# A fused linear-attention and MoE kernel: the last token tile evicted in halves by two engines, and another load time in the planner

## The chip, the cores and the metric

The kernel runs on one core of a Trainium2 chip. The metric is the device time of one execution in microseconds; less is better. The time before is the median of three runs.

## The reference, cut to what matters

```python
def _attn_ref(q, k, v, alpha):                 # each (4, 8, 768, 48): batch, heads, positions, head size
    state = np.zeros((B, H, D, D))
    for t in range(S):
        state = alpha[:, :, t, :, None] * state + np.einsum('bhd,bhe->bhde', k[:, :, t], v[:, :, t])
        y[:, :, t] = np.einsum('bhd,bhde->bhe', q[:, :, t], state)
    return y

x = attn_out.transpose(0, 2, 1, 3).reshape(3072, 384)   # tokens x (heads * head size)
h = np.maximum(x @ w_in, 0.0)                           # w_in: 384 x 2048
out = (h * h) @ w_out                                   # w_out: 2048 x 384, out: 3072 x 384 float32
```

A gated linear recurrence over 768 positions for 4 x 8 heads, and behind it a two-layer network with a squared ReLU over the 3072 tokens.

## The kernel before

**Tiles.** The 3072 tokens are 24 chunks of 128 positions, six per batch (NT = 24, NCH = 6). A chunk goes through the recurrence in closed form: the logarithm of alpha (tile `L_s`), its running sum by a matmul with a triangle of ones, the exponentials `A` and `Ainv` of it, `qA_s` = q * A and `kI_s` = k * Ainv, their transposes `qkT`, the scores `sc` (all pairs of positions), the masked scores `sm`, and the output as scores times `vb` (v in bf16) plus q times the state `sb` carried from the chunk before; `st` is that state in PSUM. The output is cast to `xn`, transposed, and lies as `xT_big` for the network. There, `w_in` matmuls fill a bank, ScalarE makes `r` = max(h, 0), VectorE squares it into `gT`, and 16 `w_out` matmuls in four quarters make one output tile, which is evicted from its bank into `ob` and stored.

The first four chunks are treated as two "super" pairs (`add_super`, u = 0 and 1), which interleave even and odd positions of 256, so that 64 rows of each of two chunks stand in one tile. The rest go through `add_chunk`, `add_scores` and `add_back`. `add_moe1` and `add_moe2` make the network; its groups of chunks have the sizes GN = 4, 1, 1, 2, 2 and so on.

**What sets the order.** Each step is an `Op` with an engine (or a choice of engines), a duration that the author gives it, the steps it depends on, a priority, and the PSUM bank that it takes and the step that gives the bank back. `Plan.run` is a list scheduler: it walks through time with these durations, and each engine takes the ready step that can start first, by priority among equals. The steps are then sorted by planned start and their instructions emitted in that order. Each engine's instruction stream is that order, and on the chip each engine works it off in order, waiting on semaphores where a tile is not ready. So a planned duration never changes how long something takes; it changes what stands ahead of what.

Loads are steps on a queue "DMA" of the plan, which is first in, first out; a load of 128 x 384 float32 takes `LD` there and is ready 2.4 us later. Stores are steps on "OUT". All loads and stores are issued by SyncE, in the one planned order. A store of a whole tile gets `.late = OUT_LATE`, 3.5 us: this is added to its planned start, so that it stands in SyncE's queue behind loads that are planned up to 3.5 us later:

```python
            op.start = t + getattr(op, "late", 0.0)
...
        self.order.sort(key=lambda o: o.start)
```

TensorE gets dummy matmuls on the tile `warm` where the plan leaves it idle near the start; the last of them stand near 22.9 us. The helper lines L251 (`mm`) and L254 (`tr`) record every matmul and transpose, L365 and L367 are ScalarE's and VectorE's branch of the helper `cast`. In `add_super`, `e_p3a` adds q times the state to the output bank `py`, `e_p3b` adds the masked scores times v, and `add_tail` casts and transposes the result.

Of the kernel before, what the change touches and what calls it, by code (L numbers as in the profile page):

```python
# [8 lines left out]
FP32 = mybir.dt.float32  # L9
# [47 lines left out]
def after(op, x=0.0):  # L57
    return (op, x)
# [86 lines left out]
def kernel(  # L145
# [10 lines left out]
    nc = tc.nc  # L156
    B, H, S, D = q.shape
    HD = H * D
    P = 128
    DP = 64  # L160
    NP = H // 2
    NCH = S // P
    d_model, d_ff = moe_w_in.shape
# [3 lines left out]
    NT = n_tok // P  # L167
# [5 lines left out]
    out_r = out.rearrange("(tt p) n -> tt p n", p=P)  # L173
# [11 lines left out]
    opool = ctx.enter_context(tc.tile_pool(name="opool", bufs=6))  # L185
# [8 lines left out]
    HF = P // 2  # L194
# [6 lines left out]
        out=utri_f, in_=ones_f, compare_op=ALU.is_ge, fill=0.0,  # L201
# [4 lines left out]
        out=sutri_f, in_=ones_f, compare_op=ALU.is_ge, fill=0.0,  # L206
# [10 lines left out]
    for src, dst in ((utri_f, half_in), (sutri_f, half_ex)):  # L217
        nc.vector.memset(dst, 0.0)
        for ab in range(2):
            h = slice(ab * HF, ab * HF + HF)  # L220
            nc.vector.tensor_copy(dst[h, h], src[h, h])
    for ab in range(2):
        h = slice(ab * HF, ab * HF + HF)
# [23 lines left out]
    def pin(ins):  # L247
        tc.keep_in_program_order(ins)

    def mm(*a, **kw):  # L250
        pin(nc.tensor.matmul(*a, **kw))  # L251
# [4 lines left out]
    plan = Plan()  # L256
# [5 lines left out]
    SUP_BANKS = sl_bank[0:4]  # L262
# [3 lines left out]
    def psum(op, shape, dt):  # L266
        i = op.slot.bank
        return banks[i].tile(shape, dt, name=f"bank{i}")
    X_SLACK = 0.2
    LD = 1.05  # L270
    LD2 = 1.51
    WLD = 2.05
    SQ_PRIO = 0.0
# [1 line left out]
    def add(eng, dur, emit, *deps, **kw):  # L275
        return plan.add(Op(eng, dur, emit, deps, **kw))
# [50 lines left out]
    LEAD = 3.5  # L327

    NS = 2
    SIDE = 1  # L330
    EITHER, SLOW = {"DVE": 0.47, "POOL": 0.95}, {"POOL": 0.95}
    KI_ON = [[EITHER, EITHER], [EITHER, EITHER]]
    ST_PRIO = -12.0
    SUP = [dict() for _ in range(NS)]

    def add_load(s, nm):
# [9 lines left out]
        prev = C[s - LB]["use_" + nm] if s - LB >= 2 * NS else None  # L346
        if 2 * NS <= s < 2 * NS + LB and (k - LB // 2) < NS:
            prev = SUP[k - LB // 2]["use_" + nm]
        d["ld_" + nm] = add("DMA", LD, ld, prev, lat=2.4)

# [12 lines left out]
    def cast(op, out_t, in_t):  # L363
        if op.eng == "ACT":
            pin(nc.scalar.copy(out_t, in_t))  # L365
        elif op.eng == "DVE":
            pin(nc.vector.tensor_copy(out_t, in_t))  # L367
        else:
            pin(nc.gpsimd.tensor_copy(out_t, in_t))

    def add_tail(s, done, first, g):
        d = C[s]

        def e_xn():
            d["xn"] = work.tile([P, HD], BF16, name="xn")
            cast(xn, d["xn"], d["py"][:, 0:HD])
        xn = add("ACT", 0.36, e_xn, done, **g)
        first.gives = xn

        def e_p4():  # L380
            d["px"] = psum(p4, [P, KT, P], BF16)
            for j in range(KT):
                tr(d["px"][:, j, :], d["xn"][:, j * P:(j + 1) * P], ident_bf)
        p4 = plan.add(Op("PE", 0.165, e_p4, [xn], takes=GLA_BANKS, lat=0.14, **g))

        def e_xT():
            cast(xT, xT_big[:, :, s * P:(s + 1) * P], d["px"])
        xT = add({"ACT": 0.36, "DVE": 0.27} if s < EARLY else "DVE", 0.27, e_xT, p4, prio=-9.0)
        d["x"] = d["end"] = xT
        p4.gives = xT  # L390
# [176 lines left out]
    def add_super(u):  # L567

        d = SUP[u]
        i = 2 * u % NBUF  # L570
        pair = (C[2 * u], C[2 * u + 1])
        L, qA, kI, ae = L_s[:, i:i + 2], qA_s[:, i:i + 2], kI_s[:, i:i + 2], ae_s[:, i:i + 2]
        old = [C[2 * u - NBUF + ab].get("end") for ab in range(2)] if u >= 2 else []
        g = dict(prio=-10.0 + u * 0.02)
        any_ = (0, 1)
# [11 lines left out]
        vb = [add("POOL", 0.55, lambda t=t: e_vb(t), d["ld_vt"], *old, prio=-5.0) for t in any_]  # L587
# [57 lines left out]
        cq = add({"DVE": 0.61, "ACT": 0.92}, 0, lambda: e_cp(cq, "qT", "pq"), p1q, **g)  # L645
# [33 lines left out]
        sm = []  # L679
# [4 lines left out]
        before = p2  # L684
# [18 lines left out]
        for ab in any_:  # L703
            s = 2 * u + ab
            c = pair[ab]
            r = slice(HF * ab, HF * ab + HF)
            before = C[s - 1].get("sb") if s else None
            if s < NCH - 1:
                def e_ps(c=c, r=r, s=s):
                    if s == 0:  # L710
                        state["ps"] = ps_st.tile([P, NP, 2 * D], FP32, name="st")
                    st = c["st"] = state["ps"]
                    for t in any_:
                        for p in range(NP):
                            mm(st[:, p, :], lhsT=kI[r, t, 2 * p:2 * p + 2, :], rhs=d["vb"][t][r, 2 * p:2 * p + 2, :],
                               start=(s == 0 and t == 0 and p == 0), stop=True, skip_group_check=True)
                ps = plan.add(Op("PE", 0.35, e_ps, [*mk, *vb, ae1, before], lat=0.16, **g))

                def e_stm(c=c, ab=ab):
                    st4 = c["st"].rearrange("p n (j e) -> p n j e", j=2)  # L720
                    pin(nc.vector.tensor_mul(st4, st4, bcast(ae[:, ab], D)))  # L721
                stm = add("DVE", 0.47, e_stm, ps, ae1, prio=ST_PRIO)

                def e_sb(c=c):
                    c["sbt"] = work.tile([P, NP, 2 * D], BF16, name="sb")
                    pin(nc.scalar.copy(c["sbt"], c["st"]))
                c["sb"] = add("ACT", 0.37, e_sb, stm, prio=-12.0)

            def e_p3a(c=c, r=r, s=s, ab=ab):
                c["py"] = psum(c["p3a"], [P, 512], FP32)  # L730
                for p in range(NP):
                    mm(c["py"][:, 2 * p * D:2 * (p + 1) * D], lhsT=d["qT"][:, p, ab].rearrange("k t c -> k (t c)"), rhs=C[s - 1]["sbt"][:, p, :],
                       start=(p == 0), stop=False, skip_group_check=True)

            def e_p3b(c=c, r=r, s=s):
                if s == 0:
                    c["py"] = psum(c["p3b"], [P, 512], FP32)
                for x in any_:
                    for hh in range(2):
                        for p in range(NP):  # L740
                            h = 2 * p + hh
                            mm(c["py"][:, h * D:(h + 1) * D], lhsT=d["sm"][x][r, hh, p, :], rhs=d["vb"][x][r, h, :],
                               start=(s == 0 and x == 0 and hh == 0 and p == 0), stop=(x == 1), skip_group_check=True)
            p3a = None
            if s:
                p3a = c["p3a"] = plan.add(Op("PE", 0.2, e_p3a, [cq, before], takes=SUP_BANKS, **g))
            p3b = c["p3b"] = plan.add(Op("PE", 0.5, e_p3b, [*sm, *vb, after(p3a)], takes=None if s else SUP_BANKS,
                                         lat=0.15, **g))
            add_tail(s, p3b, p3a or p3b, g)

    GN = [4, 1, 1, 2, 2, 2, 2, 2, 2, 2, 2, 2]
    assert sum(GN) == NT
    GT = [sum(GN[:i]) for i in range(len(GN))]
# [51 lines left out]
    def add_moe2(g, tt, before, box, quarters, pools):  # L805

        for qd in quarters:
            def e_mm(qd=qd):
                if qd == 0:
                    box["po"] = psum(box["first"], [P, 512], FP32)[:, 0:d_model]  # L810
                for kf in range(qd * FT // NQ, (qd + 1) * FT // NQ):
                    mm(box["po"], lhsT=gT[g][:, kf, tt * P:(tt + 1) * P], rhs=w_out_b[:, kf, :],
                       start=(kf == 0), stop=(kf == FT - 1))
            fs = range(qd * FT // NQ, (qd + 1) * FT // NQ) if g == 0 else range(FT)
            deps = [o for f in fs for o in sq[(g, f)]] + [w_dep("o", fs[-1] if g == 0 else FT - 1)] + ([after(before)] if before else [])
            op = plan.add(Op("PE", 0.65, e_mm, deps, takes=pools if qd == 0 else None, prio=0.1))
            op.moe = (2, 2.56 / NQ)
            if qd == 0:
                box["first"] = op
            op.lat = 0.05  # L820
            before = op
        if quarters[-1] < NQ - 1:
            return op

        def e_ev():
            box["ob"] = opool.tile([P, d_model], FP32, name="ob")
            if ev.eng == "DVE":
                pin(nc.vector.tensor_copy(box["ob"], box["po"]))
            else:
                pin(nc.scalar.copy(box["ob"], box["po"]))  # L830
        ev = add({"DVE": 0.47, "ACT": 0.38}, 0, e_ev, op, prio=-15.0)
        box["first"].gives = ev

        def e_out():
            s = GT[g] + tt
            if s >= 2 * NS:
                pin(nc.sync.dma_start(out=out_r[s], in_=box["ob"]))
            else:
                for t in range(2):
                    pin(nc.sync.dma_start(out=out2_r[s, t], in_=box["ob"][HF * t:HF * t + HF]))  # L840
        add("OUT", 0.55, e_out, ev, at=0.0).late = OUT_LATE
        return op
# [96 lines left out]
```

## Time and profile before

| | |
|---|---|
| runs shown | 189.12, 188.58, 189.08 us; median 189.08 |
| profiled execution | 187.66 us, of which the span of the core is 185.9 us |
| granted TensorE clock | 0.999 |
| TensorE matmul / weight load | 178.4 / 134.1 us busy |
| VectorE / ScalarE / GpSimd | 133.8 / 122.6 / 29.6 us busy |
| loads of 192 KB | 80, each 3.7 to 4.0 us from issue to landing (median) |
| stores of 192 KB | 20, 2.3 us; in the last 16 us 1.9 us |
| HBM | 25.17 MB read, 4.72 MB written |

The profiled execution is one run of the program under the hardware profiler; its times are counted from the start of the span. A busy time is the sum of an engine's instructions; the end of a matmul is modelled, so TensorE's holes of less than about 0.15 us do not show in it. A line "A <- B: 1.4, 2, 1.0" in the waits says that A waited for B 1.4 us in total, in 2 places, 1.0 at most. A line of the timeline is the start, the length, the engine and line, the output and inputs, and how many instructions of the kind stand together; in brackets is the idle time before it and who ended it. In a line of the groups the numbers behind the bar are the busy time in us, the mean of one in ns, and the idle time before.

### The profile page before, as it was taken

To read this page: it belongs to the slowest core of one execution; us is meant where nothing else is said; L and a number is where in the kernel's file an instruction comes from. 1 tells how busy PE (TensorE), PEld (TensorE's weight loads), DVE (VectorE), ACT (ScalarE), POOL (GpSimd) and SP (SyncE) were. 2 spreads that over 40 slices of the span, in tenths; PEclk is the share of its full clock that TensorE was granted. 3 is DMA by queue.
4 is the path that set the end of the run, shared out by engine and by line. 5 is a ranking of instruction groups with operands and counts; after the bars stand their busy time and mean duration, and the time that the engine had idled before them with its cause. 6 is when DMAs were issued, how large, how long until landed. Compare 5 with 4: busy or idle time off the path is not lost.

```text
span 185.9 us, 5105 instructions
## 1 busy us (share of the span) xinstructions
PE 178.4 (96%) x2037; PEld 134.1 (72%) x2037; DVE 133.8 (72%) x280; ACT 122.6 (66%) x282; POOL 29.6 (16%) x47
## 2 busy tenths in 40 slices
PE   6889899999999999999999999999999999999992
PEld 2666684667887878878878878777868778767761
DVE  7688679875999986876976966866987976842400
ACT  3577779455896896776676776667778668434621
POOL 5044777411012111111020020020020000000000
PEclk9999999999999999999999999999999999999999
DMA  5999999899899999999997984691011011011112
GB/s 146 261 280 339 385 370 331 175 223 205 161 206 209 236 199 231 184 231 201 189 222 162 216 166 101 157 212 61 0 42 46 2 48 42 4 42 42 46 43 84
DMA packets 99176, 30.22 MB, mean 163 GB/s; under 512 B 92112, under 2 KB 98000, under 8 KB 99152
## 3 DMA queue, kind: packets, MB, share of 16 engines
q1 hardware_dynamic: 99152, 29.89, 68.1%
q8 instruction: 16, 0.26, 0.5%
q14 instruction: 8, 0.07, 0.1%
HBM read 25.17 MB, written 4.72 MB: 161 GB/s over the span
## 4 chain that ended last, share of the span: by engine, by line
PE 88%; DMA 3%; ACT 3%; SPq 2%; DVE 1%; issue 0%
PE bank L251 77%; PE bank L254 7%; DMA at<-in_alpha_dram 3%; PE sc L251 2%; PE st L251 2%; SPq L360 2%; DVE qkT L367 1%; ACT raw L691 1%; ACT L_s L579 0%; DVE qA_s L627 0%; ACT w_in_b L304 0%; DVE st L721 0%; ACT r L790 0%; ACT ob L830 0%; ACT A L610 0%
## 5 line engine op out<-in xcount | busy, mean ns | idle before, releaser
L251 PE MATMUL bank<-xT_big,w_in_b 128*128 128x256 bf16 (+2 forms) x600 | 73.1, 269 | 0.0
L251 PE MATMUL bank<-w_out_b,gT 128*128 128x384 bf16 x384 | 72.4, 326 | 0.0
L790 ACT ACTIVATE r<-bank 128x512 bf16<-128x512 f32 x96 | 56.9, 602 | 18.8 <-PE bank L251 16.5
L251 PEld LDWEIGHTS <-w_in_b 128*128 128x128 bf16 x600 | 52.5, 98 | 9.2
L798 DVE TENSOR_TENSOR gT<-r 128x512 bf16<-128x512 bf16 x96 | 45.2, 493 | 17.1 <-ACT r L790 16.6
L251 PEld LDWEIGHTS <-gT 128*128 128x128 bf16 x384 | 35.1, 97 | 17.8
L407 POOL CAST vb<-vt 128x384 bf16<-128x384 f32 x20 | 10.9, 550 | 92.7 <-PE bank L251 45.6
L367 DVE COPY qkT<-bank 128x1024 bf16<-128x1024 bf16 (+1 forms) x26 | 16.5, 649 | 6.3 <-PE bank L254 6.2
L830 ACT COPY ob<-bank 128x384 f32<-128x384 f32 x20 | 9.6, 479 | 14.6 <-PE bank L251 14.6
L504 DVE TENSOR_TENSOR sm<-sc,utri_b 128x512 bf16<-128x512 f32 x24 | 15.4, 684 | 2.0 <-PE sc L251 2.0
L365 ACT CAST xn<-bank 128x384 bf16<-128x384 f32 x24 | 10.9, 481 | 5.8 <-PE bank L251 5.7
L440 DVE TENSOR_TENSOR qA_s<-qt,A 128x384 bf16<-128x384 f32 x20 | 11.5, 577 | 3.8 <-ACT A L421 3.7
L251 PEld LDWEIGHTS <-qkT 64*128 64x128 bf16 (+2 forms) x304 | 10.4, 98 | 4.9 <-issue 2.5
L421 ACT ACTIVATE A<-bank 128x384 bf16<-128x384 f32 x20 | 9.9, 494 | 6.2 <-PE bank L251 6.2
L367 DVE COPY xT_big<-bank 128x384 bf16<-128x384 bf16 x21 | 7.4, 354 | 8.3 <-PE bank L254 8.2
L443 DVE TENSOR_TENSOR kI_s<-kt,Ainv 128x384 bf16<-128x384 f32 x20 | 11.3, 567 | 0.0
L543 ACT CAST sb<-st 128x384 bf16<-128x384 f32 x16 | 7.6, 476 | 5.2 <-DVE st L538 5.2
L402 ACT ACTIVATE L_s<-at 128x384 bf16<-128x384 f32 x20 | 10.0, 520 | 0.5 <-DMA at<-in_alpha_dram 0.4
L504 DVE TENSOR_TENSOR sm<-bank,utri_b 128x512 bf16<-128x512 f32 x16 | 10.2, 681 | 0.0
L251 PE MATMUL bank<-warm 128*128 128x256 bf16 (+1 forms) x41 | 8.2, 333 | 2.0 <-DVE both L216 1.3
L425 ACT ACTIVATE Ainv<-bank 128x384 bf16<-128x384 f32 x20 | 9.9, 496 | 0.0
L251 PE MATMUL bank<-vb,sm 128*128 128x48 bf16 (+1 forms) x224 | 9.6, 183 | 0.0
(70 smaller groups left out, 176.3 us busy)
## 6 DMA issues: line engine op xcount, KB each, us to landing
at<-in_alpha_dram SPq DMA_DIRECT2D x20, 192.0 KB, 3.9
qt<-in_q_dram SPq DMA_DIRECT2D x20, 192.0 KB, 3.7
kt<-in_k_dram SPq DMA_DIRECT2D x20, 192.0 KB, 4.0
vt<-in_v_dram SPq DMA_DIRECT2D x20, 192.0 KB, 3.7
out_dram<-ob SPq DMA_DIRECT2D x20, 192.0 KB, 2.3
wo<-in_moe_w_out_dram SPq DMA_DIRECT2D x4, 768.0 KB, 6.8
wi<-in_moe_w_in_dram SPq DMA_DIRECT2D x3, 768.0 KB, 8.0
at<-in_alpha_dram SPq DMA_DIRECT2D x2, 384.0 KB, 4.9
```

The costliest lines, as they stand in the source:

```text
L251: pin(nc.tensor.matmul(*a, **kw))
L254: pin(nc.tensor.transpose(*a))
L365: pin(nc.scalar.copy(out_t, in_t))
L367: pin(nc.vector.tensor_copy(out_t, in_t))
L402: pin(nc.scalar.activation(L[:, :, 0:D], d["at"], AF.Ln))
L407: pin(nc.gpsimd.tensor_copy(d["vb"], d["vt"]))
L421: pin(nc.scalar.activation(d["A"], d["pm"][:, 0:HD].rearrange("p (h d) -> p h d", h=H), AF.Exp))
L440: pin(nc.vector.tensor_mul(qA[:, :, 0:D], d["qt"], d["A"]))
L443: pin(nc.vector.tensor_mul(kI[:, :, 0:D], d["kt"], d["Ai"]))
L504: pin(nc.vector.tensor_mul(d["sm"][:, hh], d["sc"][hh], utri_b.to_broadcast([P, NP, P])))
L790: pin(nc.scalar.activation(box["r"][:, 0:w], box["ph"][:, 0:w], AF.Relu))
L798: pin(nc.vector.tensor_mul(gT[g][:, f0:f0 + per, lo * P:lo * P + n], r, r))
```

## The change

Three things change.

The planner's `LD` goes from 1.05 to 0.97 us.

In `add_super`, `e_p3b` becomes one step for a list of chunks of the pair (`JOIN`, here one chunk each). The bank of the output is taken by `e_p3a` as before where there is a state to add, and otherwise by a step "NIL" that issues nothing and depends on the masked scores. `e_p3b` now waits in the plan for `e_p3a` with TensorE's planned latency of 0.13 us behind it.

In `add_moe2`, the last token tile is evicted in two halves of 192 columns, the first by VectorE and the second by ScalarE, into one tile of the same pool, and stored by two stores, the first issued by SyncE and the second by ScalarE. The first is an "OUT" step without `.late`.

```diff
-    LD = 1.05
+    LD = 0.97
...
+    JOIN = [[(0,), (1,)], [(0,), (1,)]]
...
             def e_p3a(c=c, r=r, s=s, ab=ab):
-                c["py"] = psum(c["p3a"], [P, 512], FP32)
+                c["py"] = psum(c["hold"], [P, 512], FP32)
...
+            def e_hold(c=c):
+                c["py"] = psum(c["hold"], [P, 512], FP32)
             if s:
-                p3a = c["p3a"] = plan.add(Op("PE", 0.2, e_p3a, [cq, before], takes=SUP_BANKS, **g))
-            p3b = c["p3b"] = plan.add(Op("PE", 0.5, e_p3b, [*sm, *vb, after(p3a)], takes=None if s else SUP_BANKS,
-                                         lat=0.15, **g))
-            add_tail(s, p3b, p3a or p3b, g)
+                c["hold"] = plan.add(Op("PE", 0.2, e_p3a, [cq, before], takes=SUP_BANKS, **g))
+            else:
+                c["hold"] = plan.add(Op("NIL", 0.0, e_hold, sm, takes=SUP_BANKS, lat=0.0, **g))
...
+        for abs_ in JOIN[u]:
+            p3b = plan.add(Op("PE", 0.5 + 0.1 * len(abs_) - 0.1, lambda abs_=abs_: e_p3b(abs_),
+                              [*sm, *vb, *[pair[ab]["hold"] for ab in abs_]], lat=0.15, **g))
+            for ab in abs_:
+                add_tail(2 * u + ab, p3b, pair[ab]["hold"], g)
...
+        half = d_model // 2
+        if GT[g] + tt == NT - 1:
+            def e_evh(i):
+                if "ob" not in box:
+                    box["ob"] = opool.tile([P, 2, half], FP32, name="ob2", tag="ob")
+                cast(evs[i], box["ob"][:, i], box["po"][:, i * half:(i + 1) * half])
+
+            def e_outh(i):
+                pin((nc.sync, nc.scalar)[i].dma_start(out=out_r[NT - 1, :, i * half:(i + 1) * half], in_=box["ob"][:, i]))
+            evs = []
+            for i, e in enumerate(("DVE", "ACT")):
+                evs.append(add(e, 0.28, lambda i=i: e_evh(i), op, prio=-15.0))
+            add("OUT", 0.3, lambda: e_outh(0), evs[0], at=0.0)
+            add("ACT", 0.3, lambda: e_outh(1), evs[1])
+            box["first"].gives = evs[1]
+            return op
```

More of the change, by code (lines that the diff above doesn't have):

```diff
@@ L733, in e_p3a, with e_p3b @@
                        start=(p == 0), stop=False, skip_group_check=True)
[L735 to L744, printed above, removed]
-            if s:
-                p3a = c["p3a"] = plan.add(Op("PE", 0.2, e_p3a, [cq, before], takes=SUP_BANKS, **g))
-            p3b = c["p3b"] = plan.add(Op("PE", 0.5, e_p3b, [*sm, *vb, after(p3a)], takes=None if s else SUP_BANKS,
-                                         lat=0.15, **g))
-            add_tail(s, p3b, p3a or p3b, g)
+            def e_hold(c=c):
+                c["py"] = psum(c["hold"], [P, 512], FP32)
+            if s:
+                c["hold"] = plan.add(Op("PE", 0.2, e_p3a, [cq, before], takes=SUP_BANKS, **g))
+            else:
+                c["hold"] = plan.add(Op("NIL", 0.0, e_hold, sm, takes=SUP_BANKS, lat=0.0, **g))
+        def e_p3b(abs_):
+            for x in any_:
+                for hh in range(2):
+                    for p in range(NP):
+                        h = 2 * p + hh
+                        for ab in abs_:
+                            r = slice(HF * ab, HF * ab + HF)
+                            mm(pair[ab]["py"][:, h * D:(h + 1) * D], lhsT=d["sm"][x][r, hh, p, :],
+                               rhs=d["vb"][x][r, h, :], start=(2 * u + ab == 0 and x == 0 and hh == 0 and p == 0),
+                               stop=(x == 1), skip_group_check=True)
+        for abs_ in JOIN[u]:
+            p3b = plan.add(Op("PE", 0.5 + 0.1 * len(abs_) - 0.1, lambda abs_=abs_: e_p3b(abs_),
+                              [*sm, *vb, *[pair[ab]["hold"] for ab in abs_]], lat=0.15, **g))
+            for ab in abs_:
+                add_tail(2 * u + ab, p3b, pair[ab]["hold"], g)
     GN = [4, 1, 1, 2, 2, 2, 2, 2, 2, 2, 2, 2]
```

## The prediction

> **What bounds the kernel now.** I read the page's busy times first, then TensorE's waits, the chain that ended last, and the timelines of the two places where TensorE is not yet, or no longer, at work.
>
> ```profile
> span 185.9 us, 5105 instructions
> PE 178.4 (96%) x2037; PEld 134.1 (72%) x2037; DVE 133.8 (72%) x280; ACT 122.6 (66%) x282; POOL 29.6 (16%) x47
> PE 88%; DMA 3%; ACT 3%; SPq 2%; DVE 1%; issue 0%
> ```
>
> TensorE is busy for 96% of the span and is 88% of the chain. Its waits, all of them:
>
> ```profile
> PE bank L251 <- ACT L_s L579: 1.4, 2, 1.0
> PE bank L251 <- DVE both L216: 1.3, 1, 1.3
> PE bank L251 <- ACT r L790: 0.8, 1, 0.8
> PE sc L251 <- DVE qkT L367: 0.2, 1, 0.2
> ```
>
> All lie before 20 us. From 23.2 us to the last matmul the windows view gives TensorE 159.28 busy of 159.30 us. So a new order of the middle can win only what hides inside "busy": holes between the starts of matmuls. The timeline of TensorE shows one:
>
> ```profile
> 59.97 1.15 PE L251 MATMUL bank<-xT_big,w_in_b 128*128 128x256 bf16 x9
> 61.12 0.40 PE L254 MATMUL bank<-ident_bf,qA_s 128*128 128x128 bf16 x4
> ```
>
> Nine matmuls of 256 columns that start 0.109 us apart take 0.98, so the next could start at 60.95; it starts at 61.12, 0.17 late. Read this way the holes over 0.04 us after 23.2 are at 51.7 (0.10), 54.7 (0.07), 56.8 (0.14), 60.8 (0.17), 66.7 (0.07) and 149.5 (0.12): 0.67 in all. That is the ceiling of what the middle can give.
>
> The end, from the timeline, the stores' row in the last 16 us, and SyncE's waits:
>
> ```profile
> 182.53 0.48 ACT L830 COPY ob<-bank 128x384 f32<-128x384 f32 x1 [2.12 <-PE bank L251]
> 183.03 0.33 SPq L837 DMA_DIRECT2D out_dram<-ob  x1
> DMA to landing us min/median/max: 1.8/1.9/1.9
> SPq L934 <- DMA out_dram<-ob: 1.5, 1, 1.5
> ```
>
> TensorE ends at 182.5; ScalarE evicts for 0.48; SyncE issues the last store at 183.03; it lands 1.9 later, near 184.9; closing semaphores take the last 1.0. The store of tile 22 was issued one round earlier and costs nothing.
>
> **The change, part by part.** *The end.* Two half evictions replace one. Their lengths come from two shapes of each engine:
>
> ```profile
> L830 ACT COPY ob<-bank 128x384 f32<-128x384 f32 x20 | 9.6, 479 | 14.6 <-PE bank L251 14.6
> L828 DVE COPY ob<-bank 128x384 f32<-128x384 f32 x4 | 2.2, 558 | 0.1
> L504 DVE TENSOR_TENSOR sm<-bank,utri_b 128x512 bf16<-128x512 f32 x16 | 10.2, 681 | 0.0
> ```
>
> VectorE: 681 - 558 = 123 ns for 128 columns, so 192 columns less make 558 - 185 = 0.37 us. ScalarE: its 128x512 r takes 602, the slope is again 123, so 479 - 185 = 0.29 us. If both ran at once, the halves would be ready 0.11 and 0.19 us sooner than 183.01.
>
> They do not run at once. In the built order VectorE's half waits for ScalarE's semaphore count that ScalarE's own half raises: ScalarE first, VectorE after it. No two copies out of one bank stand side by side in this trace, so what overlap would cost can't be read here. [...]
>
> Then the queue. The new SyncE store is planned without the lateness of 3.5 us that every other store has, and the order is sorted by planned start. So the last two of SyncE's queue change places: the half store of tile 23 now stands ahead of the whole store of tile 22. Tile 22, ready at 180.4, waits behind VectorE's half: ScalarE 182.53 to 182.82, hand-over 0.04, VectorE to 183.23, 0.02, half store issued 183.25 to 183.58 (0.33 as in the row), 0.03, tile 22's store issued at 183.61. Now the last issue is at 183.03, with the same 192 KB behind it: +0.58. ScalarE's own half store, issued near 182.84, is done earlier. Bounds: an eviction of VectorE of 0.28, the planner's figure, gives +0.5. Above, three stores of 384 KB in all share the DMA engines: at the 206 GB/s of a middle slice they need 1.9 us from 184.2, end at 186.1 and not 185.5, which is +1.2; at the page's best slice, 385 GB/s, they need 1.0 and stay hidden. These are large rows, so I take **+0.6**.
>
> *The start.* TensorE's output step of the first pairs is regrouped, and the plan puts three things elsewhere before 24 us. First, chunk 1's matmuls with sb now precede chunk 0's with sm. They need sb (13.20), which the st matmuls ahead of them wait for anyway. Chunk 0's xn slips by up to 0.27 us, covered by the second half of qA_s on VectorE (to 15.39), which the transposes wait for; uncovered it would cost the 0.27. Second, chunk 1's xT_big moves from ScalarE to VectorE (0.35 at 17.20), into VectorE's 0.53 us wait for the scores: nothing; beyond that gap it would cost what sticks out. Third:
>
> ```profile
> 21.56 0.48 ACT L365 CAST xn<-bank 128x384 bf16<-128x384 f32 x1
> 22.60 0.48 ACT L365 CAST xn<-bank 128x384 bf16<-128x384 f32 x1 [0.56 <-PE bank L251]
> 22.97 0.48 ACT L726 CAST sb<-st 128x384 bf16<-128x384 f32 x1
> 23.13 0.34 PE L254 MATMUL bank<-ident_bf,xn 128*128 128x128 bf16 x3
> ```
>
> ScalarE's order becomes xn, sb, xn. sb waits for VectorE's st, which ends at 22.76, so it starts at 22.80, chunk 3's xn at 23.17 (0.37 apart, as now) and ends at 23.65. Its transposes start at 23.70, not 23.13. TensorE has one group of three w_in matmuls ahead of them instead (0.33, from 22.95) and then stands from 23.28 to 23.70. Now transposes and that group are done at 23.64; then at 23.87: **+0.22**. Queued behind are ScalarE's first r of the next group, which waits for TensorE, and nothing late. Bounds 0 (if st ends earlier) and +0.5 (if the group too is late).
>
> *The middle.* The load time falls from 1.05 to 0.97. In SyncE's timeline six loads from 34.03 to 38.89 are 0.81 apart; from chunk 5's alpha (34.03) to chunk 12's (65.60), 28 loads with five tiles' stores between them, 1.13 apart. So 0.97 is too slow for loads alone and too fast with stores. The order differs from 38 to about 85 us on all engines but GpSimd and is the same on TensorE after that: L_s a place earlier on ScalarE for chunks 6 to 10, scores' neighbours and w_out groups traded on TensorE, tile 1's eviction to VectorE, tile 3's later, its store on SyncE behind chunk 10's qt. Between loads there is one store less ahead of chunks 7, 9 and 10. Chunk 8's L_s and qA_s come a place earlier, so I count the holes at 54.7 and 56.8 as gone, **-0.2**, and the one at 60.8 as left, since from chunk 9's A to its transposes the order is unchanged. Bounds: -0.67 if every hole closes, +0.9 if loads are late (below).
>
> **Sum.** +0.6 + 0.2 - 0.2 = +0.6 us on the profiled execution of 187.66 (span 185.9 and 1.7 around it): 188.3. The runs shown have a median of 189.08, 1.4 above it; the same step makes 189.7, or 0.32% more. A measurement of this kernel can tell about 0.3%, 0.57 us, from no change, so the forecast stands at that edge.
>
> **Rivals.** *Every hole closes.* Planned loads that match real ones let ScalarE and VectorE run ahead, and TensorE streams without a break from 24 us: +0.6 + 0.2 - 0.67 = +0.15, 189.2, not slower. It decides once over 0.25 us of the holes beyond my 0.2 go. For it: the plan's own idle time of TensorE in this stretch goes to nothing. Against: VectorE is 18.38 of 20 us busy from 50 to 70 us. [...] Chance 0.2.
>
> *Loads later than planned.* ScalarE works in order, and an L_s placed early blocks what is behind it. Chunk 9's alpha is issued at 53.25; with the median 3.9 it lands at 57.15, and L_s starts at 57.39, after chunk 7's xn (57.01). In the new order it stands before that xn; if the load comes no sooner, xn slips by 0.5, and TensorE, 0.3 ahead of it in slack, loses some 0.3. For chunks 7, 9 and 10 that is up to 0.9: 190.6. It decides if the store that is gone ahead of these loads (0.8 us of SyncE's issue each) does not bring them forward. Chance 0.2.
>
> *The change does what it says.* [...] The built order speaks against it. Chance 0.05.
>
> **Numbers.** My case has 0.55; it spans +0.3 to +0.9, 60% of it above 0.57. Slower: 0.33 + 0.2, and 0.02 for a dearer end: 0.55. Faster: 0.05, as runs spread by 0.3%. Same: 0.40. The range goes from the closing of most holes, 189.0, to late loads, 190.5.
>
> **What would show it.** Right: SyncE's last issue near 183.6 to 183.9, a whole tile behind a half one, VectorE's half starting after ScalarE's ends, TensorE's end within 0.4 of 182.5, transposes of xn at 23.7. Wrong: halves side by side; a wait of ScalarE on alpha between 45 and 62 us; TensorE ending over 0.5 earlier, which would need holes I did not see.

## The result, and the profile after

The changed kernel takes 190.84 us (median of 6 runs, 189.68 to 191.27); the kernel before, timed beside it, 188.81 us (6 runs, 187.84 to 189.12). The ratio is 1.0106, with a 95% interval of 1.0065 to 1.0147. So the change costs about 2.0 us. The prediction had the sign, but said +0.6 us and a range of 189.0 to 190.5. Here and below, ratios leave out single runs that took over 1.5% longer than the fastest of their kernel; medians and ranges do not.

The profiled execution of the changed kernel took 190.91 us with a span of 189.2, against 187.66 and 185.9 before: 3.3 us more. The top of its page, and the shares of its chain:

```profile
span 189.2 us, 5113 instructions
PE 180.4 (95%) x2036; PEld 135.6 (72%) x2037; DVE 134.4 (71%) x281; ACT 122.2 (65%) x282; POOL 29.5 (16%) x47
PE 88%; ACT 4%; DVE 2%; DMA 2%; issue 1%
```

TensorE is 2.0 us busier than before for the same matmuls, and the remaining 1.3 us are idle. Its waits:

```profile
PE bank L251 <- DVE both L216: 1.3, 1, 1.3
PE bank L254 <- ACT xn L366: 1.1, 2, 0.8
PE bank L251 <- ACT L_s L580: 0.8, 1, 0.8
PE bank L251 <- ACT r L798: 0.8, 1, 0.8
```

The second line is new. The end of the timeline of the changed kernel:

```profile
185.15 0.32 ACT L366 COPY ob<-bank 128x192 f32<-128x192 f32 x1 [2.12 <-PE bank L251]
185.49 0.38 ACTq L841 DMA_DIRECT2D out_dram<-ob  x1
185.50 0.36 DVE L368 COPY ob<-bank 128x192 f32<-128x192 f32 x1 [7.10 <-ACT ob L366]
185.88 0.33 SPq L841 DMA_DIRECT2D out_dram<-ob  x1
186.31 0.41 SPq L862 DMA_DIRECT2D out_dram<-ob  x1
```

ScalarE's half comes first, VectorE's half waits for it, and the last issue of SyncE is the whole store of tile 22 at 186.31. From the end of TensorE's last matmul (185.11) to the end of the span it is 4.08 us; before it was 3.43. That is **+0.65 at the end**. The other 2.6 us are lost ahead of TensorE's last matmul, and the lag of single matmuls behind the same ones of before tells where: the first matmul with w_in is 1.37 us late, the 25th 2.46, and from 120 us on it stays at 2.6 to 2.7. So nearly all of it is there by 27 us.

The first 1.37 us were in no step of the prediction. The start of TensorE's timeline, before:

```profile
6.27 1.47 PE L251 MATMUL bank<-warm 128*128 128x256 bf16 x12
7.57 0.67 PE L254 MATMUL bank<-ident_bf,qA_s 128*128 128x128 bf16 x8
```

and after:

```profile
6.74 2.72 PE L251 MATMUL bank<-warm 128*128 128x256 bf16 x12
9.25 1.02 PE L254 MATMUL bank<-ident_bf,qA_s 128*128 128x128 bf16 x8
```

Up to here TensorE has the same instructions in the same order in both. Twelve dummy matmuls take 1.47 us before and 2.72 after. The distance of their starts is 109 ns before and 213 after. In the execution of before TensorE ran at half rate (427 ns for 512 columns) to 4.2 us and at full rate from 5.42 on; in that of after it ran at half rate until 10.05 us. The windows view of after does not show it (the figures behind the busy times are the granted clock, 1.00, the DMA share and GB/s):

```profile
7.00:9.30 2.30, 2.30 (x13) 1.61 (x12) 1.66 (x4) 1.01 (x4) 0.38 (x1) 1.00 1.28 261
```

The trace has no row of the granted clock ahead of 10.09 us, and the view counts a stretch without a row as 1.00; in the trace of before the first row, at full clock, begins at 4.73 us.

So the first question of the experiments was whether the 1.37 us belong to the change.

### The profile page after: what moved, and what is told of

Its sections match the earlier page's. It is cut to its first block, busy times and chain, and to the rows that moved or that the text cites. A ratio compares the mean times of both kernels' runs of the same rounds, so it can differ in the third digit from the quotient of the medians.

```text
span 189.2 us, 5113 instructions
## 1 busy us (share of the span) xinstructions
PE 180.4 (95%) x2036; PEld 135.6 (72%) x2037; DVE 134.4 (71%) x281; ACT 122.2 (65%) x282; POOL 29.5 (16%) x47
## 4 chain that ended last, share of the span: by engine, by line
PE 88%; ACT 4%; DVE 2%; DMA 2%; issue 1%
PE bank L251 76%; PE bank L254 7%; PE sc L251 3%; PE st L251 2%; DMA at<-in_alpha_dram 2%; DVE qkT L368 1%; ACT r L798 1%; ACT xn L366 0%; ACT sb L727 0%; ACT L_s L580 0%; ACT w_in_b L304 0%; ACT raw L692 0%; DVE st L722 0%; ACT L_s L403 0%; ACT Ainv L426 0%
## 5 line engine op out<-in xcount | busy, mean ns | idle before, releaser
L806 DVE TENSOR_TENSOR gT<-r 128x512 bf16<-128x512 bf16 x96 | 46.7, 506 | 15.7 <-ACT r L798 15.0
L251 PE MATMUL bank<-warm 128*128 128x256 bf16 (+1 forms) x41 | 9.4, 376 | 2.0 <-DVE both L216 1.3
```

The lines of the kernel that those rows point to most:

```text
L806: pin(nc.vector.tensor_mul(gT[g][:, f0:f0 + per, lo * P:lo * P + n], r, r))
```

## The experiments

Where the text below says "nine dummies", the seven matmuls of 512 columns at the start of the kernel are nine. "Lag" is how late a matmul, or TensorE's end, is against before with nine dummies. The kernels were timed in four groups, each on another chip and beside runs of the kernel before (medians 188.52, 188.63, 188.89 and 188.71 us); a ratio is against these. One execution of each kernel was traced, so what is read from a timeline is read from one.

### The rate at the start

Before with nine, ten and four dummies, and the changed kernel with nine and four:

```diff
     wp = banks[4].tile([P, 512], FP32, name="bank4")
-    for _ in range(7):
+    for _ in range(9):
         mm(wp, lhsT=warm[:, 0:P], rhs=warm, start=True, stop=True)
```

> The kernel before with nine dummy matmuls of 512 columns at the start instead of seven; nothing else differs. In the profiled execution of before TensorE works at full rate (109 ns for 256 columns) from 5.42 us on, in that of after at half rate (214 ns) until 10.05 us, though up to there the two programs are the same; in both it stands idle for 0.8 to 1.0 us after the seven dummies. Theory A (the rate at the start is drawn by each execution, and a gap in the dummies makes the slow draw likelier): nine dummies end near 5.1 us, the slow stretch ends by 7.5 us at the latest, the spread of the times falls from 1.3 us to under 0.7 us and the median from 188.8 to 187.7-188.2 us. Theory B (the late start belongs to the changed program): nothing changes here, 188.5-189.1 us with the old spread.

> The changed kernel with nine dummy matmuls instead of seven. Theory A: 189.2-189.9 us, under the 190.8 us with seven, and 1.3 to 1.9 us above before with nine; the first w_in matmul at 17.8-18.3 us instead of 19.21. Theory B: 190.5-191 us, first w_in matmul still at 19.2. By the terms of the prediction alone (tail +0.6, start +0.2, middle -0.2) it would be 0.6 us above before with nine: 188.3-188.8 us.

> Before with four dummy matmuls instead of seven: TensorE is idle from about 3 to 5.3 us and should start at half rate nearly always. Theory A: 189.0-189.8 us, at the slow end of before's own times (187.5-189.6), the first w_in matmul near 19.2 instead of 17.85 us. Rival (the rate does not depend on the dummies): as before, 188.5.

> The changed kernel with four dummies. Theory A: 190.6-191.6 us, the slow end of its own times. If the late start also meets GpSimd's casts (gT on VectorE 1.5 us instead of 0.4 near 21 and 23 us, and sb ahead of xn on ScalarE passing that on, 1.0 us of stall near 25 us), the changed kernel loses more by the late start than before does: 2.2-2.6 us between the two with four dummies against 1.8 with nine. If that stall was an accident of one execution: 1.6-1.9.

> Before with ten dummies. Theory A: 187.5-187.8 us, as with nine (187.6) or a little less, with a spread under 0.6 us but for single runs; one dummy more delays the first scores by 0.1 us at most. Rival (nine was a lucky number or chip): 188-188.6.

| kernel | dummies | median us (range, runs) | ratio to before, 95% | full rate from | first w_in matmul |
|---|---|---|---|---|---|
| before | 9 | 187.60 (187.43 to 189.48, 12) | 0.9970 [0.9941, 0.9999] | 4.2 us | 17.75 us |
| before | 10 | 187.72 (187.55 to 189.15, 12) | 0.9966 [0.9940, 0.9991] | 7.2 us | 17.98 us |
| before | 4 | 189.44 (188.46 to 190.88, 12) | 1.0049 [1.0018, 1.0080] | 9.8 us | 19.13 us |
| changed | 9 | 189.39 (189.23 to 190.58, 7) | 1.0084 [1.0053, 1.0114] | 5.4 us | 17.90 us |
| changed | 4 | 191.19 (190.74 to 193.36, 6) | 1.0161 [1.0113, 1.0209] | 11.2 us | 19.82 us |

The first w_in matmul stood at 17.85 in the profiled execution of before and at 19.21 in that of after. Theory A holds. The 1.37 us are what an execution loses that starts at half rate, and the change has no part in them. The kernel before loses the same with four dummies (19.13). With nine or ten its times draw together, 10 of 12 within 0.5 us each time, where the kernel before beside them was spread from 187.5 to 189.6 and to 190.7. Nine do not always bring full rate at 5.4 us; in other kernels with nine below TensorE was still at half rate until 6.2 to 7.3 us, but the first w_in matmul was then only 0.2 us late.

One forecast failed here. Between the medians of the changed kernel and of before lie 1.75 us with four dummies, about as much as with nine, and not the 2.2 to 2.6 expected if the late start costs the changed kernel more. With times spread over 2.4 and 2.6 us and 6 runs of the one, this does not decide it; the two traces of late starts do show an extra loss (below).

In the traces of before and after the row of the full clock begins where the distance of the matmul starts halves: at 4.73 us, between the starts at 3.78 and 5.42, and at 10.09 us, between those at 10.00 and 10.10. It lasts 180.91 us in before and 177.49 in after. Up to the change of rate the same instructions ran in both, and both began with 427 ns for 512 columns; what sets the moment was not shown. The step of 1.37 us is 0.7% of this kernel.

With nine dummies on both sides the change costs 189.39 - 187.60 = 1.79 us, in the spans of the traces 187.5 - 185.7 = 1.8. What follows takes these 1.8 us apart.

### The end

Halves alone, and halves alone with SyncE's half store as late in the plan as every other store:

```diff
-            add("OUT", 0.3, lambda: e_outh(0), evs[0], at=0.0)
+            add("OUT", 0.3, lambda: e_outh(0), evs[0], at=0.0).late = OUT_LATE
```

> Before with nine dummies and, of the change, only the last tile's eviction in halves with two stores. The prediction's tail term: 0.6 us more than before with nine dummies (0.4 to 0.9), SyncE's last issue the whole store of tile 22 near 0.6 us later relative to TensorE's end, everything ahead of it as before. Rival (the halves run at once, stores hidden): 0.2 us less.

> Halves alone (with nine dummies), but SyncE's half store planned with the lateness of 3.5 us that every other store has, so that the whole store of tile 22 goes out ahead of it. The prediction's tail working: of the 0.6-0.7 us that the halves cost, the swapped stores make 0.36-0.45, the serial eviction (VectorE's half after ScalarE's) the other 0.2-0.25: so 0.2 to 0.3 us above before with nine dummies, 187.8-187.9. Rival (the serial halves are the whole cost): 188.2-188.4 as without the lateness.

Halves: 188.38 us (188.06 to 188.88, 12 runs), 0.78 over before with nine dummies; from TensorE's end to the span's end 4.09 us against 3.43. With the lateness: 188.18 us (187.62 to 188.50, 12), on another chip; from TensorE's end to the span's end 3.37. The timelines, first halves alone:

```profile
182.85 0.36 DVE L367 COPY ob<-bank 128x192 f32<-128x192 f32 x1 [7.10 <-ACT ob L365]
183.24 0.33 SPq L833 DMA_DIRECT2D out_dram<-ob  x1
183.66 0.40 SPq L854 DMA_DIRECT2D out_dram<-ob  x1
```

and with the lateness:

```profile
180.67 0.33 SPq L854 DMA_DIRECT2D out_dram<-ob  x1
183.12 0.36 DVE L367 COPY ob<-bank 128x192 f32<-128x192 f32 x1 [7.10 <-ACT ob L365]
183.50 0.33 SPq L833 DMA_DIRECT2D out_dram<-ob  x1
```

The halves are as serial as before, but the whole store (L854) is back at 180.67, and the end costs nothing: the whole of the 0.66 us was the swap of two stores. I had expected 0.2 to be left for the serial halves. It is not, since the last store is issued 0.23 later after TensorE's end (0.77 against 0.54) but lands in 1.63 us, where a whole tile takes 1.86. By its median alone, 0.6 over 187.60, the rival (188.2 to 188.4) could hardly be told apart. But the 0.6 does not come from the end: in the profiled execution TensorE's end lagged by 0.45, 0.30 of it after 27 us, with two waits of ScalarE on alpha (1.2 us) that the execution of before with nine dummies does not have.

### The start and the middle

The rest of the change without the halves, its two parts alone, and the load time moved the other way:

```diff
-    LD = 1.05
+    LD = 0.97    # joinld_w9 (with the regrouped steps), ld_w9 (alone)
+    LD = 1.13    # ldslow_w9 (alone); join_w9 keeps 1.05 and has the regrouped steps
```

> Before with nine dummies and the rest of the change (TensorE's output steps regrouped, load time 0.97), last eviction whole. The prediction's terms: start +0.2, middle -0.2, so the same as before with nine dummies within 0.3 us. Rival (start and middle were mis-sized, whatever the start's rate): 0.8 to 1.3 us more, with a stall of TensorE of about 1 us near 24 us on xn behind sb.

> Before with nine dummies and, of the change, only the planned load time 1.05 -> 0.97. Theory M (the middle term of the prediction has the wrong sign: with shorter planned loads L_s and r stand so early in ScalarE's order that a load that lands late stops ScalarE and then TensorE): before with nine dummies +0.3 to +1.0 us, 187.9-188.6, and a wide spread (over 1 us) because the landing differs from run to run; start as before. The prediction's term: -0.2 us, 187.4. Rival (the regrouping makes the middle dear): within 0.2 us of 187.6.

> Before with nine dummies and, of the change, only the regrouped output steps of TensorE (load time 1.05, whole last eviction). The prediction's start term: +0.2 us at 24 us. Theory M: the middle costs no more than in before, so 187.8 (187.6-188.1) with a spread under 0.8 us. Rival (the regrouping makes the middle dear, by the other places it gives the steps from 38 us on): 188.3-189.0.

> Before with nine dummies and the planned load time raised to 1.13, the mean that SyncE's timeline shows with stores between the loads. Theory M: ScalarE's L_s stand no earlier than the loads land, the holes of 0.36-0.55 us between 50 and 70 us shrink: 187.1-187.6 with a narrow spread. Rival (any reshuffle of the middle order is as good as random): anywhere in 187.3-188.6.

| kernel, nine dummies | median us (range) | ratio to before, 95% | lag at 27 us | 27 us to TensorE's end | ScalarE's waits on alpha, 38 to 100 us |
|---|---|---|---|---|---|
| regrouped, 0.97 | 188.92 (188.06 to 190.66) | 1.0041 [1.0011, 1.0072] | 0.34 | +0.30 | none |
| all of the change | 189.39 (189.23 to 190.58) | 1.0084 [1.0053, 1.0114] | 0.21 | +0.94 | 0.9 in 1 |
| 0.97 alone | 190.39 (189.55 to 190.86) | 1.0087 [1.0053, 1.0121] | 0.11 | +2.00 | 2.9 in 5 |
| regrouped alone | 189.10 (188.50 to 190.06) | 1.0021 [0.9995, 1.0047] | 0.32 | +0.97 | 0.4 in 1 |
| 1.13 alone | 188.82 (188.65 to 189.29) | 1.0004 [0.9978, 1.0029] | 0.11 | +1.74 | 0.6 in 1 |

Lags are those of the profiled executions, the medians those of all runs. The profiled execution is the shortest of its kernel in the first three rows and the longest in the last, so the loss of the middle is probably more than shown in those three and less in the last. At 27 us the kernels without the regrouping lag by 0.11 and those with it by 0.21 to 0.34, so the regrouping makes the start 0.1 to 0.2 us dearer, about as predicted. The middle is dearer in every row, and most with the smaller load time alone, where the prediction had counted 0.2 us less. Raising the load time does not help either, so theory M's forecast for it (187.1 to 187.6) was wrong: TensorE stands there at several places behind VectorE's xT_big (0.8 us in two waits). With the regrouping alone it stands behind an xT_big too, 0.45 us in a hole of 0.61 us at 70.8 us. The medians lie above what I had expected in every row: 0.97 alone 190.39, not 187.9 to 188.6; regrouped alone 189.10, where theory M had 187.6 to 188.1 and its rival 188.3 to 189.0; both together 1.3 over before with nine, as the rival had it (0.8 to 1.3), but without its stall near 24 us. A new order cost something whichever way the planner was pushed. What follows explains it for the load time 0.97; for the other two rows it stays open.

Two holes of TensorE come with 0.97 in every execution, also where no load is late. One is 0.29 us at 44 us: a running-sum matmul (bank<-L_s,utri_b) follows after four w_out matmuls, where before has eight and then the scores, and starts at 44.52, just after VectorE's copy of qkT has ended (44.38); that it waits for the bank which this copy empties is inferred. The other is 0.20 to 0.29 us at 62 us, behind an r of ScalarE. The holes of before at 54.7 and 56.8 (0.07 and 0.14) are gone, as predicted.

The rest is loads. A load of alpha is `at<-in_alpha_dram`; L_s is made from it. The changed kernel with nine dummies, at 66 us:

```profile
61.16 0.57 SPq L346 DMA_DIRECT2D at<-in_alpha_dram  x1
65.89 0.52 ACT L403 ACTIVATE L_s<-at 128x384 bf16<-128x384 f32 x1 [0.94 <-DMA at<-in_alpha_dram]
66.31 1.07 ACT L798 ACTIVATE r<-bank 128x512 bf16<-128x512 f32 x2
66.94 0.49 PE L251 MATMUL bank<-xT_big,w_in_b 128*128 128x256 bf16 x3 [0.45 <-ACT r L798]
```

and the same place without the halves:

```profile
60.87 0.65 SPq L346 DMA_DIRECT2D at<-in_alpha_dram  x1
64.95 0.54 ACT L403 ACTIVATE L_s<-at 128x384 bf16<-128x384 f32 x1
65.42 1.25 ACT L798 ACTIVATE r<-bank 128x512 bf16<-128x512 f32 x2
```

The alpha of the first took 4.70 us from issue to landing, that of the second 3.74. L_s waits for it, two r stand behind L_s in ScalarE's order, and TensorE's next w_in group needs the bank that the first r frees: it starts 0.61 us late. Before's order meets late alphas too, but has other steps behind them. The same place in the kernel with the late half store, where TensorE lost 0.30 us after 27 us in all:

```profile
64.97 1.25 ACT L790 ACTIVATE r<-bank 128x512 bf16<-128x512 f32 x2 [0.50 <-PE bank L251]
67.01 0.52 ACT L402 ACTIVATE L_s<-at 128x384 bf16<-128x384 f32 x1 [0.78 <-DMA at<-in_alpha_dram]
```

Here two r stand ahead of the L_s that waits, and with 0.97 two stand behind it. So it is this place, more than the wait, that makes a late alpha dear: before with ten dummies waited 0.9 us for two alphas and lost 0.04 us. This is read from the orders; no run moves L_s alone.

To see whether the loads make the difference, the k loads of chunks 4 to 23 were left out, with the order of everything else kept:

```diff
         def ld():
+            if nm == "kt":
+                return
...
-            pin(nc.vector.tensor_mul(kI[:, :, 0:D], d["kt"], d["Ai"]))
+            pin(nc.vector.tensor_mul(kI[:, :, 0:D], d["qt"], d["Ai"]))
```

> The changed kernel with nine dummies, without the loads of k for chunks 4 to 23 (kI is formed from q there, so the sums differ from the reference); the plan and the order of all other instructions are kept, and SyncE has 20 of its 80 later loads fewer. Theory M (of the middle's +0.95 us in the profiled execution the +0.6 at 66 us is an L_s that waits 0.94 us for a late alpha with two r behind it, and the spread of the times comes from there; the holes at 44 and 62 us, 0.5 us, are the order's own): no wait of ScalarE on alpha, 188.6-189.0 us instead of 189.39, the holes at 44 and 62 us still there. Rival (the loads do not matter, the order alone costs): 189.2-189.6.

> Before with nine dummies and load time 0.97, again without the loads of k for chunks 4 to 23. With them ScalarE waited 2.9 us for alpha in five places and the time was 190.39 us, TensorE 2.1-2.2 us behind before. Theory M: the waits on alpha go, and with them the hole of 1.06 us at 75 us and part of the others: 188.2-189.0 us. Rival (the order alone): 189.9-190.5.

With load time 0.97 alone: 187.82 us (187.72 to 188.14, 12 runs; ratio to before 0.9946 [0.9924, 0.9969]) instead of 190.39. The alpha that had been issued at 70.87 and landed at 75.44, under a wait of 1.3 us and a hole of 1.06, was now issued at 67.19 and landed at 70.98; ScalarE waited for no alpha between 38 and 100 us, TensorE lost 0.33 after 27 us instead of 2.00, and the spread fell from 1.3 to 0.4 us. The changed kernel: 189.01 us (188.88 to 189.27, 12) instead of 189.39, at the upper edge of what was expected, with no wait on alpha; TensorE lost 0.57 after 27 us, 0.28 of it past 149 us, and the two holes of the order stood where they were. So with 0.97 the order's own holes cost about 0.3 us net of the holes that went, and the loads the rest. Executions with 0.97 side by side (the two with edits to the start are told below):

| execution with load time 0.97 | ScalarE's waits on alpha, 38 to 100 us | 27 us to TensorE's end |
|---|---|---|
| changed kernel, as timed first | none | +0.33 |
| regrouped, nine dummies | none | +0.30 |
| 0.97 alone without k | none | +0.33 |
| all of the change, nine | 0.9 | +0.94 |
| all of the change, four | 1.8 | +1.76 |
| all of the change, four, GpSimd's casts cut | 2.1 | +1.88 |
| all of the change, nine, with two mends | 2.3 | +2.31 |
| 0.97 alone, nine | 2.9 | +2.00 |

Five executions of before's order, with seven, nine, ten and four dummies and with halves, lie between 0.0 and +0.2, and the one with the late half store at +0.3. What makes an alpha late in one execution and not in the next was not settled: from 38 to 100 us their median time from issue to landing lies between 3.7 and 4.1 us in all of them, the longest between 4.0 and 6.0. Both parts vary. The alpha above was issued 0.29 us later than without the halves and took 0.96 us longer; the one issued at 70.87 was issued 1.57 us later than its like without the halves (69.30) and took about as long.

### Why the start costs 1.0 and not 0.2

With nine dummies the regrouping costs 0.1 to 0.2 us by 27 us, but the profiled execution of the changed kernel lost 1.1 between 19 and 27 us beyond its late start. Its timeline there (L300 is GpSimd's cast of the weights):

```profile
21.14 1.46 POOL L300 CAST w_in_b<-wi 128x1536 bf16<-128x1536 f32 x1
21.35 1.53 DVE L806 TENSOR_TENSOR gT<-r 128x512 bf16<-128x512 bf16 x1
22.76 1.47 POOL L300 CAST w_in_b<-wi 128x1536 bf16<-128x1536 f32 x1 [0.16 <-DMA wi<-in_moe_w_in_dram]
23.05 1.45 DVE L806 TENSOR_TENSOR gT<-r 128x512 bf16<-128x512 bf16 x1 [0.17 <-ACT r L798]
24.42 0.55 DVE L722 TENSOR_TENSOR st<-st,ae_s 128x384 f32<-128x384 f32 x1
25.01 0.48 ACT L727 CAST sb<-st 128x384 bf16<-128x384 f32 x1 [1.61 <-DVE st L722]
25.38 0.48 ACT L366 CAST xn<-bank 128x384 bf16<-128x384 f32 x1
25.92 0.34 PE L254 MATMUL bank<-ident_bf,xn 128*128 128x128 bf16 x3 [0.85 <-ACT xn L366]
```

A gT takes 0.42 us alone. Here two take 1.5, each ending 0.27 to 0.28 after a cast of w_in by GpSimd that began before it. st follows on VectorE, sb waits 1.61 us for st, and xn stands behind sb: the order xn, sb, xn that the prediction had priced at +0.22. In before the two casts began at 20.54 and 22.56, each after a wait for its load, so in the late start they moved by only 0.60 and 0.20 us. The two gT, at 19.98 and 21.69 before, moved by 1.37, onto the casts. The same place in before with four dummies, which starts as late:

```profile
22.97 1.43 DVE L798 TENSOR_TENSOR gT<-r 128x512 bf16<-128x512 bf16 x1 [0.17 <-ACT r L790]
23.89 0.48 ACT L365 CAST xn<-bank 128x384 bf16<-128x384 f32 x1 [0.57 <-PE bank L251]
24.42 0.34 PE L254 MATMUL bank<-ident_bf,xn 128*128 128x128 bf16 x3
24.91 0.48 ACT L726 CAST sb<-st 128x384 bf16<-128x384 f32 x1 [0.55 <-DVE st L721]
```

The same slow gT, but xn is ahead of sb, and the transposes lose 0.13 us, as they do in before with seven and with nine. The changed kernel with four dummies has the stall of after: 0.99. Two edits of it tell the links apart, the order of ScalarE and the casts:

```diff
     plan.run(gate)
+    plan.order.remove(C[3]["sb"])
+    plan.order.insert(plan.order.index(C[3]["xn_op"]) + 1, C[3]["sb"])
```

> The changed kernel with four dummies (late start); one instruction moved by hand: ScalarE's sb of chunk 3 stands behind chunk 3's xn, as in before; all else in the same order. Theory S (gT is late on VectorE, so st and sb are late, and xn stands behind sb): the stall of 0.99 us ahead of xn's transposes near 25.4 us falls to 0.1-0.2 us, as in before with four dummies; first later w_in matmuls 0.8 us earlier, the whole 190.3-190.8 us against 191.2 (the late alpha of the middle can hide part). Rival (TensorE would wait for something else there, st or xT_big): stall still over 0.6 us, 191.0-191.4.

```diff
-                pin(nc.gpsimd.tensor_copy(dst, box["w"]))
+                if which == "i":
+                    pin(nc.gpsimd.tensor_copy(dst[:, :, 0:32], box["w"][:, :, 0:32]))
+                    pin(nc.gpsimd.memset(dst[:, :, 32:], 0.01))
+                else:
+                    pin(nc.gpsimd.tensor_copy(dst, box["w"]))
```

> The changed kernel with four dummies; GpSimd's three casts of w_in read only 96 of 1536 columns and fill the rest of the tile with a constant by a memset (so most of w_in is left out of the sums). Theory P (VectorE's gT, with two inputs, does not run beside a GpSimd instruction that reads, and waits for its end): the gT near 22.0 and 23.7 us take 0.4-0.6 us instead of 1.53 and 1.43, the stall ahead of xn's transposes falls from 0.99 to about 0.2 us, the whole 190.3-190.8 us. Rival (any GpSimd work, writes too, or the loads' traffic slows gT): gT stays at 1.3-1.6 us, stall and time as with four dummies, 191.0-191.4.

xn first: the gT still take 1.53 and 1.43 us, and the stall falls from 0.99 to 0.36, of which 0.19 is now a wait for VectorE's xT_big. That is the larger part, not the 0.8 expected. The time, 191.01 us (189.38 to 192.60, 6 runs), does not tell it from 191.19, nor does its ratio, 1.0105 [1.0051, 1.0160] against 1.0161 [1.0113, 1.0209]. The profiled execution is the longest of the six; what it loses more lies in the middle, 2.56 us, with two waits on alpha of 2.3 us in all.

Casts cut: 190.57 us (189.88 to 191.85, 6), and no stall at all. But this execution reached full rate at 8.5 us and not at 11.2, so its first two gT (20.68 and 22.38, both 0.42) met hardly anything of GpSimd, and the missing stall proves little. What it does show is a gT beside each kind of GpSimd's work:

```profile
24.97 1.30 POOL L302 MEMSET w_in_b<- 128x1440 bf16 x1
25.57 0.43 DVE L810 TENSOR_TENSOR gT<-r 128x512 bf16<-128x512 bf16 x1 [0.60 <-ACT r L802]
26.93 1.70 POOL L304 CAST w_out_b<-wo 128x1536 bf16<-128x1536 f32 x1 [0.66 <-DMA wo<-in_moe_w_out_dram]
27.53 1.37 DVE L810 TENSOR_TENSOR gT<-r 128x512 bf16<-128x512 bf16 x1 [0.23 <-ACT r L802]
```

Wholly inside a memset it takes 0.43 us; begun inside a cast, 1.37, to 0.27 after the cast's end. So theory P's forecast for a gT beside a cast and beside a memset holds in these four lines (1.37 and 0.43 us). By what means a cast holds a gT up, and whether gT's two inputs matter, was not shown.

Last, both mends together, with nine dummies:

> The changed kernel with nine dummies, ScalarE's sb of chunk 3 behind xn, and SyncE's half store with the lateness of the other stores. If the terms add up: 189.39 - 0.65 (tail) - 0.15 (start) = 188.5-188.7 us, what is left over before with nine dummies (187.6) being the middle's 0.3-0.95; its spread stays about 1 us. Rival (the terms hide each other): above 188.9.

189.64 us (188.88 to 191.74, 12 runs; ratio to before 1.0046 [1.0008, 1.0083]), not the 188.6 expected. In its profiled execution the mends did their part: 3.38 us from TensorE's end to the span's end, a lag of 0.17 at 27 us. The middle took it back: 2.31 us, with waits on alpha of 2.3, and holes of 1.01 at 66 us and 0.68 at 76 us. So the terms do not simply add up: while an alpha may be late, a mend elsewhere can be hidden. The version that beats both kernels is before with nine or ten dummies, 187.6 to 187.7 us.

## Why the prediction was wrong, step by step

With nine dummies on both sides the traces give +0.2 for the start, +0.94 for the middle and +0.65 for the end, 1.8 us, where the prediction's sum was +0.2, -0.2 and +0.6. That the forecast had the sign rests on the end alone.

**The end** was right. +0.6 was forecast, +0.65 was measured in the changed kernel and +0.66 for halves alone, with each sign in place: ScalarE's half first, a whole tile's store behind a half one, the last issue 1.20 us after TensorE's end, where 1.1 was worked out. The rival with both halves at once is out. No run shows halves at once: VectorE's half began 0.03 us after ScalarE's had ended, at 185.50 in the changed kernel and at 182.85 in halves alone. Nor does any run show that the length of the rows matters, which decided between +0.6 and +1.2: in the changed kernel the three last stores landed in 1.6 to 1.9 us. Only the working had a share too many: it put part of the 0.6 on the serial halves, and all of it belongs to the swapped stores, because a half store lands 0.23 us sooner.

**The start** was right in mechanism, and in size only where TensorE starts at full rate: +0.22 forecast, 0.1 to 0.2 with nine dummies. The term was sized on one execution, with gT at 0.42 and 0.60 us and st at 22.76. In a late start the same order passes on two gT of about 1.5 us: a stall of 1.0 us in both traces of it (seven and four dummies), twice the bound of +0.5. That is the step that failed in the profiled execution of the changed kernel, +1.1 for +0.22. The row "gT 0.60" in before, beside 0.42 for the one at 19.98, was the sign that gT meets something there: it ended 0.29 us after a cast.

**The middle** is the step that failed once the start's rate is evened out: -0.2 forecast, +0.94 measured with nine dummies. "Chunk 8's L_s and qA_s come a place earlier, so I count the holes at 54.7 and 56.8 as gone, **-0.2**": they went, but the step looked only at the holes that were there. The new order brings 0.29 at 44 us and 0.24 at 62 us of its own, +0.3 net of the two that went, and beyond that what late alphas cost, from nothing to 2.0 us. The rival "Loads later than planned" named this mechanism exactly (L_s blocks what is behind it in ScalarE's order), but had a chance of 0.2, a price of 0.3 for each load and a sum of 0.9 at most. A single late alpha cost up to 1.46 us (four dummies). Its sign, a wait on alpha between 45 and 62 us, was looked for a little too early: the waits that cost most stand at 66 to 76 us.

**The base** failed too. "The same step makes 189.7" carried a sum worked out on the profiled execution, one with an early start, over to the median, 1.4 us above it, as if the distance had no part in the change. Most runs of before are probably late ones: of its 112 runs beside the experiments 21 took under 188 us, near the profiled 187.66. In a late execution the change costs 1.0 at the start, not 0.2. In the two profiled executions the 3.3 us are 1.4 for the rate, 1.1 for the start, 0.1 to 0.2 for the middle (against this execution of before) and 0.65 for the end. How the 2.0 us between the medians divide, with late and early starts on both sides, can't be read from one trace of each.

## What to carry to other kernels

Before pricing anything, ask why the profiled time differs from the median; here the distance between the starts of the dummies after 6 us (109 and 213 ns) told of two kinds of execution, and two or three more of them at the start won 0.9 to 1.0 us, half of what the change costs. An instruction that waits for a load, moved forward on an engine that works in order, can make everything behind it as late as the latest load (at 66 us a wait of 0.94 us for alpha became a hole of 0.61 in TensorE), so look at what stands behind it now and price it by the longest landing, not by the median, and by several executions. When a step is added to a planner, see that it gets the same marks as its like: one missing lateness swapped two stores and cost 0.66 us.

## What the runs showed of the hardware

TensorE's half rate at the start does not show in the windows view, which reads 1.00 there in both executions. The distances of matmul starts (213 against 109 ns for 256 columns) tell it, and so does the place where the trace's rows of the granted clock begin (4.73 and 10.09 us). From 1.25 to 4.2 us busy, then idle for 0.8 to 1.0 us, TensorE was at full rate by 5.4 us in one execution and only at 10.05 us in another; with nine or ten dummies it was by 7.3 us in every profiled execution. A gT took 0.42 us alone, 0.43 inside a memset of GpSimd and 0.47 to 1.68 when it began inside GpSimd's cast of w_in or w_out, each time to 0.27 to 0.29 us after the cast's end. At the end of the kernel a store of 96 KB landed in 1.63 to 1.69 us and one of 192 KB in 1.84 to 1.93, so half the bytes won only 0.2 us there.
